# Attention and a squared-ReLU FFN: two units' rest rows stored and multiplied as one pair in the last unit, a new order of the second product, piece differences on VectorE

## The chip, the core and the metric

The kernel runs on one core of a Trainium2 chip. Its time is the device time of one execution in microseconds; "before" is the median of three runs. Five engines work side by side, each through its own instructions in order: TensorE (PE, matrix products into the eight PSUM banks; PEld are its weight loads), VectorE (DVE), ScalarE (ACT), GpSimd (POOL) and SyncE (SP), which here issues nearly all DMAs.

## What is computed

```python
# q, k, v: (8, 12, 448, 64); g_q, g_k: (64,); w_in: (768, 2048); w_out: (2048, 768); all fp32
q_n, k_n = rmsnorm(q, g_q), rmsnorm(k, g_k)
attn = softmax(q_n @ k_n^T / sqrt(64))
x = (attn @ v) as (3584, 768)          # 8 batches of 448 tokens, 12 heads of 64
h = maximum(x @ w_in, 0)
out = (h * h) @ w_out
```

## The kernel before

The eight batches form four **units** of two batches (u = 0 to 3). While a unit's FFN runs, the attention of the next two batches is worked in between: `run` draws pieces of the FFN from a generator (`ffn`) until a planned cost is spent, then a **visit** puts in the attention of the next pair of heads (`visit_among`, `visit_whole`). `place` gives the cost at which each visit comes; in units 1 and 2 there are three visits to each block. The last unit (u = 3) has no attention beside it.

A unit's FFN has four **blocks** (`NBLK`), each with a quarter of the hidden features. A block has two stages:

- The **first product** x @ w_in. Unit 0 uses seven products in place of eight on 2 x 2 parts (`first_products`, matmuls of 448 columns, L971); units 1 to 3 apply the same scheme twice (`deep_products`, matmuls of 224 columns, L1027). The weights for that, ten pieces each of seven forms, are derived in unit 0 (`deep_steps`, `derive`): ten sums for each of four blocks and each of two slices of forms, five and five, L1403. Two of each five (pieces 5 and 9) run on POOL, three on DVE. Each result goes into one of four buffers ("more") and is stored to DRAM by SP (L1421) before the buffer is used again; one step is taken at each `yield` of the stream.
- The **second product** (h*h) @ w_out (`second_products`). Tokens of a batch are 448 = 3 x 128 + 64. For each of three token tiles `tt` the first batch's 128 tokens and the second batch's are the upper and lower half of a seven-product scheme (P1 to P7, table `PRODUCTS`, L1212, each product two contraction steps of 128x384). Its left operands S1, S2, S4 and S3 are sums that POOL makes of the hidden values (`hidden_sum`, L1136). The results are added by DVE into accumulators in SBUF (`add_to`, L1269 and L1239; in a unit's first block ACT or DVE copies instead).
- The **rests**, 64 tokens of each batch, together 128 rows, are multiplied plainly: four parts by two halves of columns, eight matmuls a block (`multiply_rest`, L1150), into an accumulator of their own.

In units 1 to 3 the first tile of a block follows `FIRST_OF_BLOCK = P1, rest0, P5, P4, P6, P2, rest1, P3, P7`, where the two rest steps use banks 1 and 2 and stand where POOL still makes the sums; the other tiles follow `SECOND_ORDER = P1, P2, P5, P6, P4, P3, P7`. Three banks serve the products by turns (`roles`). P1 is issued before the last step of the first product. The tasks of attention on POOL and elsewhere are held back until the sums, or the rests, are through (`held`).

SP's queue has the loads of attention, of weights (`load_piece` L891, `load_out` L901) and the stores of results (`store`, L1274) in the order in which the program issues them; `later` delays an issue by a number of steps. An engine's queue is in order: a waiting instruction holds those behind it.

Of the kernel before, what the change touches and what calls it, by code (L numbers as in the profile page):

```python
# [14 lines left out]
F32 = mybir.dt.float32  # L15
# [3 lines left out]
ALU = mybir.AluOpType  # L19
# [3 lines left out]
P = 128  # L23
# [201 lines left out]
def program(ctx, tc, rows, v, g, wide, ones, moe_w_in, moe_w_out, out, shift):  # L225

    nc = tc.nc
# [687 lines left out]
    FIRST_ORDER = ["P1", "P5", "P2", "P6", "P3", "P4", "P7"]  # L915
    FIRST_OF_BLOCK = ["P1", "rest0", "P5", "P4", "P6", "P2", "rest1", "P3", "P7"]
    SECOND_ORDER = ["P1", "P2", "P5", "P6", "P4", "P3", "P7"]
    COST_IN, COST_OUT, COST_DEEP = 12 * NK // 2, 10, 3
    COST_SECOND = (NT * 7 + 4) * COST_OUT
    COST = NF // 2 * 7 * COST_IN + NBLK * COST_SECOND  # L920
    LATER = NBLK * (7 * 11 * COST_DEEP + COST_SECOND)

# [6 lines left out]
    def ffn(u):  # L931

        accs = []
        for blk in range(NBLK):

            hid = [
                ffn_p.tile([P, 2, 2, S], F32, name="hid", tag=f"hid{a}", bufs=1) for a in range(2)
            ]
            sums_ = [
                ffn_p.tile([P, 2, NT * P], F32, name="sums", tag=f"S{n}", bufs=1) for n in range(3)  # L940
            ]
            second = second_products(u, blk, hid, sums_, accs)
            if u:
                yield from deep_products(u, blk, hid, sums_, second)
            else:
                for t in range(2):
                    products = first_products(u, 2 * blk + t, [a[:, t] for a in hid])
                    for n, cost in enumerate(products):
                        if t and n < 4:
                            hidden_sum(hid, sums_, 0, n)  # L950
                        if t and blk == NBLK - 1:
                            let_go(u, PRODUCTS[FIRST_ORDER[n]][3])
                        yield cost
                make_all_deep()
                if blk == NBLK - 1:
                    for n in range(4):
                        load_piece(n, False)
                        load_piece(n, True)
            yield from second
# [184 lines left out]
    def multiply_rest(u, blk, hid, places, some, acc=None, halves=range(2)):  # L1144

        w_sb = [out_sb[n] for n in out_of(u, blk)]
        for half in halves:
# [7 lines left out]
            if acc is not None:  # L1155
                add_to(acc[:, ts(half, HALF)], ps, blk == 0)

    def second_products(u, blk, hid, sums_, accs):

        if blk == 0:  # L1160
            accs.extend(new_acc() for _ in range(2 * NT + 1))
        flat = [a.rearrange("p t e s -> p t (e s)") for a in hid]
        ns = out_of(u, blk)
        w_sb = [out_sb[n] for n in ns]
# [14 lines left out]
            turn_roles(2, 1, 0)  # L1179

        def store_rows(tt, e):
            if tt is None:
                parts = [(2 * u, P * NT, REST), (2 * u + 1, 0, REST)]
            else:
                parts = [(2 * u + e, REST * e + P * tt, P)]
            store(accs[-1 if tt is None else 2 * tt + e], parts)

        to_store = deque([(None, 0)])
        final = u == B // 2 - 1
        (a11, s3), (a12, a22) = [(a[:, :, LOWER], a[:, :, UPPER]) for a in flat]  # L1190
        lefts = {"11": a11, "12": a12, "22": a22, "S1": s1, "S2": s2, "S3": s3, "S4": s4}
        for tt in range(NT):
            upper_acc, lower_acc = accs[2 * tt], accs[2 * tt + 1]
            c11, c12 = [upper_acc[:, ts(h, HALF)] for h in range(2)]
            c21, c22 = [lower_acc[:, ts(h, HALF)] for h in range(2)]
            order = SECOND_ORDER if tt or not u else FIRST_OF_BLOCK
            engine = nc.scalar if order is SECOND_ORDER else nc.vector
            for name in order:
                if name.startswith("rest"):
                    a = int(name[-1])  # L1200
# [5 lines left out]
                        held.discard("others")  # L1206
                    yield 2 * COST_OUT
                    continue
                role, first, left, right = PRODUCTS[name]
                ps = roles[role][:, 0:HALF]  # L1210
                for t in range(2):
                    nc.tensor.matmul(  # L1212
                        ps, lhsT=lefts[left][:, t, ts(tt, P)], rhs=w_sb[t][:, OUT.index(right), :],
                        start=first and t == 0, stop=t == 1,
                        skip_group_check=not first,
                    )
                if name == "P1":
                    add_to(c11, ps, blk == 0, engine)
                    if order is FIRST_OF_BLOCK:
                        make_sums(0, 1)  # L1220
                        yield COST_OUT
                        make_sums(2, 3)
                        held.discard("pool")
                        continue
                elif name == "P5":
                    add_to(c22, ps, blk == 0, engine)
                elif name == "P2":
                    add_to(c11, ps)
                elif name == "P6":
                    add_to(c12, ps, blk == 0, engine)  # L1230
                elif name == "P4":
                    if blk == 0 and engine is nc.scalar:
                        nc.scalar.mul(c21, ps, -1.0)
                    elif blk == 0:
                        nc.vector.tensor_scalar(
                            out=c21, in0=ps, scalar1=-1.0, scalar2=None, op0=ALU.mult
                        )
                    else:
                        nc.vector.tensor_tensor(out=c21, in0=c21, in1=ps, op=ALU.subtract)  # L1239
                elif name == "P3":  # L1240
                    add_to(c12, ps)
                else:
                    add_to(c21, ps)
                    add_to(c22, ps)
                    to_store.append((tt, 1))
                if name == "P3":
                    to_store.append((tt, 0))
                if name in ("P2", "P4") and blk == NBLK - 1:
                    while to_store and order is not FIRST_OF_BLOCK:
                        store_rows(*to_store.popleft())  # L1250
                yield COST_OUT
            turn_roles(2, 0, 1)
        while to_store and blk == NBLK - 1:
# [132 lines left out]
    def deep_steps(blk, upper, lower):  # L1386
# [11 lines left out]
        def derive(some, n, left, right, op):  # L1398
            size = some.stop - some.start
            made[n] = ffn_p.tile([P, 4, P], F32, name="more", tag="more", bufs=4)[:, 0:size]  # L1400
            left, right = [x() for x in (left, right)]
            engine = nc.gpsimd if n in (5, 9) else nc.vector
            engine.tensor_tensor(out=made[n], in0=left, in1=right, op=op)  # L1403
            to_keep.append((keep[:, some, PLACES[n]], made[n]))

        to_keep, steps = deque(), []
# [94 lines left out]
    def place(u, x):  # L1501
# [1 line left out]
        if u == 0:  # L1503
            return COST * x / unit
        block = LATER // NBLK
        second = block - COST_SECOND
        offsets = (second * 3 // 7, second + 9 * COST_OUT, second + 22 * COST_OUT)
        at = [0] + [b * block + some for b in range(NBLK) for some in offsets]
        at[-1] = LATER
        n, more = divmod(x / VISITS, 1)  # L1510
# [67 lines left out]
    def new_acc():  # L1578
        return ffn_p.tile([P, DM], F32, name="acc", tag="acc", bufs=2 * NT + 1)
# [247 lines left out]
```

## Time and profile before

| | us |
|---|---|
| time, median of three runs (1410.63 to 1413.95) | 1411.15 |
| time of the profiled execution | 1414.61 |
| its span, first to last instruction | 1412.7 |
| ACT busy (42%) | 587.9 |
| POOL busy (57%) | 802.0 |
| matmuls of first products L971 and L1027 (xT) | 131.6 and 289.5 |
| matmuls of second products L1212 (hid and sums) | 271.3 and 205.6 |

The span is counted from the first instruction; stretches and starts are in us from there. Unit 0's FFN lies at about 110 to 500, unit 1's at 505 to 835, unit 2's at 835 to 1160 and unit 3's at 1160 to 1407. An fp32 matmul leaves two records each of PE and PEld. Records of PE overlap, so a row's mean is longer than the distance from one to the next.

DMA sizes and times to landing, from the list of DMA issues: out_sb 1536 KB 9.7 us; in_sb 384 KB 4.0 us; x_rows 224 KB 3.7 us; out_dram 384 KB 3.1 us and 192 KB 2.8 us; in_deep from "more" 256 KB 2.8 us and 192 KB 3.8 us.

### The profile page before, as it was taken

Reading aid. Unit: us, or ns where it says so; the run is one execution under the profiler, and the core shown is the slowest. Engines: PE = TensorE matmul, PEld = TensorE weight load, DVE = VectorE, ACT = ScalarE, POOL = GpSimd, SP = SyncE. Lnnn points to the kernel's source line nnn. Section 1 sums busy time; section 2 is a strip of 40 time slices with the busy share of each in tenths; the row PEclk is TensorE's granted clock in tenths of the full one; section 3 lists DMA queues with packets and bytes.
Section 4 is the critical chain, followed back from the end, with each engine's and each line's share of the span. In section 5 each row is a group of like instructions: output and inputs, shape, how many; then the busy total and the mean of one; then the engine's idle time right before and its main releaser. Section 6 shows DMA issues by size and latency. Waiting matters only on the chain.

```text
span 1412.7 us, 19458 instructions
## 1 busy us (share of the span) xinstructions
PE 1373.6 (97%) x6336; PEld 849.9 (60%) x6336; DVE 847.8 (60%) x1659; ACT 587.9 (42%) x1126; POOL 802.0 (57%) x794
## 2 busy tenths in 40 slices
PE   7999999999999999999999999999999999999998
PEld 3333444444444466685766767576676868778694
DVE  4998565987888764355455765454554564344443
ACT  6775566645646234442343434343342403121230
POOL 5668855755756877475575877565574554030311
PEclk9999999999999999999999999999999999999999
DMA  5556746867759875382646747374641726324132
GB/s 144 144 146 179 202 106 170 234 176 195 241 136 267 253 219 167 76 267 66 198 134 200 186 122 257 85 206 123 189 136 44 254 71 231 126 91 175 45 146 81
DMA packets 378931, 229.15 MB, mean 162 GB/s; under 512 B 271940, under 2 KB 347588, under 8 KB 374724
## 3 DMA queue, kind: packets, MB, share of 16 engines
q1 hardware_dynamic: 378528, 227.75, 55.6%
q8 instruction: 52, 0.85, 0.2%
q14 instruction: 59, 0.48, 0.1%
q10 hardware_dynamic: 292, 0.07, 0.0%
HBM read 172.49 MB, written 55.25 MB: 161 GB/s over the span
## 4 chain that ended last, share of the span: by engine, by line
PE 78%; POOL 5%; issue 4%; DMA 4%; DVE 3%; SPq 2%; ACT 2%; POOLq 0%; DVEq 0%; ACTq 0%
PE bank L1212 30%; PE bank L1027 20%; PE bank L971 7%; PE bank L1150 5%; PE bank L549 4%; PE bank L434 4%; PE bank L445 4%; PE bank L535 3%; POOL sum L472 2%; DMA words<-in_moe_w_in_dram 1%; DMA qk<-in_k_dram 1%; DMA words<-in_moe_w_out_dram 1%; POOL rr L203 1%; PE bank L610 1%; PE bank L570 1%
## 5 line engine op out<-in xcount | busy, mean ns | idle before, releaser
L1027 PE MATMUL bank<-xT,in_sb 128*128 128x224 f32 x1344 | 289.5, 354 | 5.1 <-ACT part L1016 2.5
L1212 PE MATMUL bank<-out_sb,hid 128*128 128x384 f32 x768 | 271.3, 490 | 6.6 <-DVE acc L1269 4.8
L1269 DVE TENSOR_TENSOR acc<-acc,bank 128x384 f32<-128x384 f32 x324 | 173.3, 549 | 170.6 <-PE bank L1212 141.2
L1027 PEld LDWEIGHTS bank<-xT,in_sb 128*128 128x128 f32 x1344 | 252.5, 190 | 17.4 <-ACT wT L453 5.6
L453 ACT ACTIVATE wT<-bank,rr 128x448 f32<-128x448 f32 x288 | 164.4, 632 | 170.7 <-PE bank L434 99.9
L1212 PEld LDWEIGHTS bank<-out_sb,hid 128*128 128x128 f32 x768 | 144.9, 191 | 111.9 <-DVE acc L1269 8.6
L1212 PE MATMUL bank<-out_sb,sums 128*128 128x384 f32 x576 | 205.6, 489 | 1.5 <-DVE acc L1269 1.4
L203 POOL TENSOR_TENSOR rr<-ms,minus_half 128x8 f32<-128x8 f32 (+1 forms) x96 | 147.3, 1535 | 76.6 <-DVE ms L196 73.1
L1012 DVE TENSOR_TENSOR hid<-hid,bank 128x224 f32<-128x224 f32 x312 | 111.1, 383 | 86.4 <-PE bank L1027 82.5
L1212 PEld LDWEIGHTS bank<-out_sb,sums 128*128 128x128 f32 x576 | 107.9, 190 | 85.4 <-issue 4.8
L971 PE MATMUL bank<-xT,in_sb 128*128 128x448 f32 x336 | 131.6, 545 | 0.0
L472 POOL TENSOR_TENSOR sum<-sum,wT 128x448 f32<-128x448 f32 (+1 forms) x96 | 112.1, 1189 | 9.6 <-ACT wT L453 8.1
L1080 POOL TENSOR_TENSOR hid<-hid 128x448 f32<-128x448 f32 x24 | 27.3, 1144 | 158.2 <-DVE hid L1012 153.8
L445 PE MATMUL bank<-qT,kT 64*128 64x448 f32 (+1 forms) x492 | 104.6, 571 | 3.5 <-ACT qT L368 2.0
L472 POOL TENSOR_TENSOR sum<-wT 128x448 f32<-128x448 f32 x48 | 57.5, 1220 | 88.3 <-ACT wT L453 88.3
L971 PEld LDWEIGHTS bank<-xT,in_sb 128*128 128x128 f32 x336 | 62.2, 190 | 68.6 <-issue 62.8
L1150 PE MATMUL bank<-out_sb,hid 128*128 128x384 f32 x256 | 87.6, 488 | 0.0
L1084 ACT ACTIVATE hid<-hid 128x448 f32<-128x448 f32 x96 | 55.0, 573 | 69.6 <-DVE hid L1012 48.5
L1027 PE MATMUL bank<-more,in_sb 128*128 128x224 f32 x288 | 76.1, 357 | 1.5 <-DVE hid L1022 1.5
L434 PE MATMUL bank<-qT,kT 64*64 64x448 f32 x552 | 75.7, 541 | 1.9 <-ACT wT L453 1.9
L180 ACT ACTIVATE squares<-qk 128x512 f32<-128x512 f32 (+1 forms) x68 | 39.4, 579 | 88.6 <-POOL xT L689 51.1
L445 PEld LDWEIGHTS bank<-qT,kT 64*128 64x128 f32 (+1 forms) x492 | 35.8, 166 | 65.7 <-issue 40.8
(136 smaller groups left out, 2037.5 us busy)
## 6 DMA issues: line engine op xcount, KB each, us to landing
out_sb<-out_forms SPq DMA_DIRECT2D x24, 1536.0 KB, 9.7
in_sb<-in_deep SPq DMA_DIRECT2D x64, 384.0 KB, 4.0
in_sb<-in_deep SPq DMA_DIRECT2D x80, 256.0 KB, 3.9
words<-in_moe_w_in_dram SPq DMA_DIRECT2D x32, 384.0 KB, 3.6
words<-in_moe_w_out_dram SPq DMA_DIRECT2D x32, 384.0 KB, 3.6
out_forms<-out_sb SPq DMA_DIRECT2D x8, 1536.0 KB, 6.8
qk<-in_q_dram SPq DMA_DIRECT2D x96, 96.0 KB, 2.6
qk<-in_k_dram SPq DMA_DIRECT2D x96, 96.0 KB, 2.7
```

The costliest lines, as they stand in the source:

```text
L203: self.nc.gpsimd.tensor_tensor(out=self.rr[i][:, x, 0 : self.count(i)], in0=ms, in1=self.minus_half.to_broadcast(list(ms.shape)), op=ALU.pow,)
L434: nc.tensor.matmul(sc[ds(half * D, D)], lhsT=turned[i, 1][ds(e * D, D), ds(m * P + half * D, D)], rhs=turned[i, 0][ds(e * D, D), :], start ...
L445: nc.tensor.matmul(sc[some], lhsT=turned[p, 1][r, keys], rhs=turned[p, 0][r, :], start=True, stop=True,)
L453: nc.scalar.activation(new_weights((i, m), e), sc, AF.Exp, scale=rows.rr[i][:, 1, 2 * m + e : 2 * m + e + 1],)
L472: nc.gpsimd.tensor_tensor(out=sums[i, e][some], in0=left[some], in1=weights[key_of(i, m), e][some], op=ALU.add)
L549: nc.tensor.matmul(bank[ds(e * D, D), :], lhsT=values[i][keys, n, e, :], rhs=weights[(i, n), e][keys], start=n == 0, stop=n == NJ - 1 and ...
L971: nc.tensor.matmul(ps, lhsT=w_sb[:, IN.index(left), c, :], rhs=forms[u, c][right], start=first and c == 0, stop=c == NK - 1, skip_group_ch ...
L1012: nc.vector.tensor_tensor(out=quarter(name, n), in0=quarter(base, n), in1=ps, op=ALU.add)
L1027: nc.tensor.matmul(ps, lhsT=left, rhs=right, start=start, stop=stop, skip_group_check=True)
L1150: nc.tensor.matmul(ps, lhsT=hid[a].rearrange("p t e s -> p t (e s)")[:, t, ds(NT * P, P)], rhs=w_sb[t][:, 2 * a + half, :], start=(a, t) = ...
L1212: nc.tensor.matmul(ps, lhsT=lefts[left][:, t, ts(tt, P)], rhs=w_sb[t][:, OUT.index(right), :], start=first and t == 0, stop=t == 1, skip_g ...
L1269: nc.vector.tensor_tensor(out=acc, in0=acc, in1=ps, op=ALU.add)
```

## The change

Three things change.

1. **Rests of units 1 and 2** (`KEPT`) are no longer multiplied there. `keep_rests` stores the 128 rest columns of both hidden tiles to DRAM, two DMAs of 128 KB for each block. In the last unit `bring_rests` loads the same block's rests of both units at the block's start into tiles that attention no longer uses, and `add_rests` makes the four sums on POOL (128x256). The rests of unit 1 are the upper half and those of unit 2 the lower half of a fourth tile (`tt == NT`), which runs the seven products in `SECOND_ORDER` behind the three others. Its accumulators lie in the tiles of q and k rows, and its rows are stored at the end. Units 0 and 3 multiply their own rests as before.
2. **Units 1 and 2 follow `SPLIT_ORDER`**, 21 products of all three tiles in one list, each with a number of its bank: five banks (the three of `roles` and banks 1 and 2) until P2 of the first tile, then three, while one of the five goes back to attention in exchange (`roles[:], banks[1] = ...`). The costs in `place` follow: visits come at 7 and 18 products after the first product's end instead of 9 and 22.
3. **Pieces 5 and 9** in `derive` run on DVE instead of POOL: 16 sums of 128x512 and 128x384.

```diff
+    SPLIT_ORDER = [
+        ("P1", 0, 0), ("P1", 1, 3), ("P4", 0, 2), ("P5", 0, 1), ("P4", 1, 4), ("P6", 0, 0),
+        ("P2", 0, 2), ("P3", 0, 1), ("P7", 0, 0), ("P6", 1, 3), ("P2", 1, 1), ("P5", 1, 0),
+        ("P1", 2, 1), ("P3", 1, 0), ("P7", 1, 3), ("P2", 2, 0), ("P6", 2, 1), ("P5", 2, 3),
+        ("P4", 2, 0), ("P3", 2, 3), ("P7", 2, 1),
+    ]
-    LATER = NBLK * (7 * 11 * COST_DEEP + COST_SECOND)
+    COST_SHORT = NT * 7 * COST_OUT
+    LATER = NBLK * (7 * 11 * COST_DEEP + COST_SHORT)
+    KEPT = range(1, B // 2 - 1)
+    kept = {u: dram.tile([NBLK, P, 2, 2, P], F32, name=f"rests{u}") for u in KEPT}
+    extra = {}
...
             second = second_products(u, blk, hid, sums_, accs)
+            if u == B // 2 - 1:
+                bring_rests(blk)
+                add_rests()
...
+    def keep_rests(u, blk, hid):
+        for a in range(2):
+            nc.sync.dma_start(
+                kept[u][blk, :, a],
+                hid[a].rearrange("p t e s -> p t (e s)")[:, :, ds(NT * P, P)],
+            )
+    def bring_rests(blk):
+        if not extra:
+            for name in ("11", "12", "S3", "22", "S1", "S2", "S4"):
+                some = att.tile([P, S], F32, name="wT", tag="wT", bufs=8)
+                extra[name] = some[:, 0 : 2 * P].rearrange("p (t n) -> p t n", t=2)
...
+        for u, names in zip(KEPT, (("11", "12"), ("S3", "22"))):
+            for a, name in enumerate(names):
+                nc.sync.dma_start(extra[name], kept[u][blk, :, a])
+    def add_rests():
...
+            (s1, a21, a22, ALU.add), (s2, s1, a11, ALU.subtract),
+            (s4, a12, s2, ALU.subtract), (a21, a11, a21, ALU.subtract),
+        ):
+            nc.gpsimd.tensor_tensor(out=dst, in0=left, in1=right, op=op)
...
+        if split:
+            places = [*roles, banks[1], banks[2]]
+            for name, tt, n in SPLIT_ORDER:
+                engine = nc.scalar if tt and n < 3 else nc.vector
+                product(tt, name, places[n][:, 0:HALF], engine)
+                if (name, tt) == ("P1", 0):
+                    yield from sums_behind_first()
+                    continue
+                if (name, tt) == ("P2", 0):
+                    roles[:], banks[1] = [places[0], places[3], places[1]], places[2]
+                    held.discard("others")
+                    later.append([3, lambda: keep_rests(u, blk, hid)])
+                if tt:
+                    store_some(name)
+                yield COST_OUT
+        for tt in range(0 if split else NT + final):
...
-            engine = nc.gpsimd if n in (5, 9) else nc.vector
-            engine.tensor_tensor(out=made[n], in0=left, in1=right, op=op)
+            nc.vector.tensor_tensor(out=made[n], in0=left, in1=right, op=op)
...
-        second = block - COST_SECOND
-        offsets = (second * 3 // 7, second + 9 * COST_OUT, second + 22 * COST_OUT)
+        second = block - COST_SHORT
+        offsets = (second * 3 // 7, second + 7 * COST_OUT, second + 18 * COST_OUT)
```

## The prediction

> **What bounds the kernel now.** I read the engine totals first, then the chain of waits, then the engines' busy time stretch by stretch, and last the timeline where something waits.
>
> ```profile
> span 1412.7 us, 19458 instructions
> PE 1373.6 (97%) x6336; PEld 849.9 (60%) x6336; DVE 847.8 (60%) x1659; ACT 587.9 (42%) x1126; POOL 802.0 (57%) x794
> L1150 PE MATMUL bank<-out_sb,hid 128*128 128x384 f32 x256 | 87.6, 488 | 0.0
> ```
>
> PE is the bound over the whole span: 97%. The L1150 row is the rests' multiplication, the work that the change cuts: 256 records in four units of four blocks, 16 in each block (8 matmuls, two records to each fp32 matmul). Its mean of 488 ns is not what one costs, since matmuls overlap; the chain of waits in the last unit gives that:
>
> ```profile
> 1262.83 20.64 PE bank L1212 x64
> 1283.47 28.55 PE bank L1027 x150
> 1324.39 20.64 PE bank L1212 x64
> ```
>
> 64 records of 128x384 back to back take 20.64 us, 0.3225 us each. These rows join without a gap: a block of the last unit is pure PE time (1262.83 to 1324.39, 61.56 us). By stretch:
>
> ```profile
> 345.00:369.00 24.00, 21.96 (x75) 8.75 (x74) 23.59 (x32) 17.09 (x34) 22.34 (x18) 1.00 0.88 252
> 440.00:462.00 22.00, 22.00 (x74) 9.65 (x73) 21.59 (x30) 12.60 (x24) 16.99 (x16) 1.00 0.94 279
> 600.00:700.00 100.00, 99.08 (x556) 70.42 (x555) 52.35 (x112) 38.06 (x73) 58.91 (x58) 1.00 0.63 183
> 1200.00:1300.00 100.00, 100.00 (x410) 77.14 (x410) 41.35 (x88) 19.75 (x41) 12.98 (x12) 1.00 0.35 126
> ```
>
> Columns: stretch, its length, then busy PE, PEld, DVE, ACT, POOL. In the second unit (600 to 700) PE is 99% busy with DVE at half; in the last PE is full. Only in the first unit is another engine full: DVE is busy 98% of 345 to 369 and 440 to 462, and there PE does wait:
>
> ```profile
> PE bank L1212 <- DVE acc L1269: 6.2, 5, 2.2
> PE bank L445 <- ACT qT L368: 2.0, 1, 2.0
> PE bank L1212 <- POOL out_sb L1443: 1.8, 1, 1.8
> ```
>
> All of these lie in the first unit: 277.39 (0.31), 281.66 (1.42), 285.76 (2.17), 380.22 (0.92) and 469.61 (1.43) for the accumulators, 367.81 for qT, 472.30 for out_sb.
>
> **The product count (part 1).** Units 2 and 3 lose their rests: 2 units x 4 blocks x 16 = 128 records x 0.3225 = 41.28 us. The last unit gains one pair by seven products: 4 blocks x 7 products x 2 contraction steps x 2 records = 112 x 0.3225 = 36.12 us. Net -16 records, **-5.16 us**. Both sides stand on the path at full price: in units 2 and 3 PE is 98 to 99% busy, in the last unit 100%. Seven products for eight is all that the arithmetic can give.
>
> **What part 1 adds elsewhere.** Stores: 2 per block of two units, 128 KB each, 16 in all, on SP. They read hid, which the next block writes first about 14 products (18 us) and a whole attention visit later; x_rows stores of 224 KB land in 3.7 us. SP does block (10.5 us from 570.12), but the stores stand ahead of that load in the new order. Loads: 4 per block of the last unit, 128 KB; in_sb loads of 128 KB land in 3.0 us. In blocks 2 to 4 they wait at SP for the previous pair to leave PE, and the in_sb loads queued behind them are four to five pieces ahead of PE (a piece is 22 records, 4.2 us), so some 16 us cover them. POOL: 4 sums of 128x256 per block, at most the 1.0 us of the 128x384 rows (L1136), so 4 us, used first about 56 us later. Only in the first block do T3 and T4 pieces (L718, until 1167.8) queue behind them and the load: 3 us + 4 us takes them to about 1175, and PE needs T3 at its sixth piece, 1160.2 + 5 x 4.2 = 1181. Cover 6 us. DVE: 8 evictions of 0.55 us in 9.03 us of PE, 4.4 us: hidden. Tail: the last row store becomes two of 192 KB (2.8 us to landing) for one of 384 KB (3.1); one more issue at some 0.4 us against 0.3 us. Together **0**, ends 0 and +1.5.
>
> **The new order of the second product (part 2).** PE has no stall in the old second products of units 2 and 3 above the 0.7 us restart after a visit, so nothing can be gained. What can be lost is bank reuse. Eviction time:
>
> ```profile
> 554.92 1.45 PE L1212 MATMUL bank<-out_sb,sums 128*128 128x384 f32 x4
> 556.41 0.56 DVE L1267 COPY acc<-bank 128x384 f32<-128x384 f32 x1 [1.27 <-PE bank L1212]
> ```
>
> From a product's first matmul to the end of its eviction is 2.05 us (556.97 - 554.92). The old order always had two other products (2 x 1.29 us) between two uses of a bank: free 1.8 us early. The new order has only one between P2 and P1 of the next tile, P5 and P3, P3 and P2: reuse at 2.58 us, 0.5 us early. That is 3 places x 8 blocks = 24. DVE runs strictly in order, so whatever stands ahead of these evictions counts: the qT and kT transposes (two of 0.6 us), a reduce with its scaling (0.55 + 0.17), the transposes of the inverse (0.65, held by POOL: at 659.57 it waited 1.08). Following the new order, most long ones fall after an eviction that has two products of room; the transposes after P2 put P5's eviction 0.5 us late, just at the margin. Two thirds of the places keep their margin and one third loses about 0.1 us: **+1**. Ends: 0, and 24 x 0.25 = +6 if DVE is typically 0.7 us late. The sums for P5, P6, P3 and P7 come no later relative to PE: P5 still stands 2.58 us behind P1's neighbour (two products instead of half the rests), and the visit now lies between P2 and P3, so S4 (ready at 557.5) and S3 (559.4) are in time. Visits come 2.6 us closer twice a block; POOL, which feeds them, idles 4.5 to 7.6 us before each, so it stays covered, and if not, each visit could cost the missing part (in the +6).
>
> **Piece differences (part 3).** 16 sums leave POOL (mean 1.3 us, 21 us) for DVE. What one costs on DVE: 0.55 us alone, 0.65 median, so 16 x 0.6 = 9.7 us more on an engine that is full in two stretches. Against it stands what POOL's sums do to DVE:
>
> ```profile
> 350.09 1.58 POOL L1403 TENSOR_TENSOR more<-in_sb 128x512 f32<-128x512 f32 x1
> 350.46 1.42 DVE L1342 TENSOR_SCALAR out_sb<-words 128x384 uint32<-128x384 uint32 x1
> 351.81 0.61 DVE L1113 TENSOR_TENSOR hid<-bank,part 128x448 f32<-128x448 f32 x1
> ```
>
> L1342's median is 0.354 us; beside a POOL sum it took 1.42, while L1113, which reads PSUM, kept its 0.61. Summed over all DVE instructions that overlap a POOL piece, time above their usual duration is 16.4 us: 1 us per piece. In 345 to 369: relief 4.6 us, added 2.4; in 440 to 462: 4.1 against 2.4; around 259 to 272: 2.0 against 1.8. So DVE reaches qT of 367.81 some 2.2 us sooner (PE's wait of 2.0 goes; next late there is PE itself) and the accumulator of 469.61 1.7 us sooner (1.4 goes; the wait for out_sb at 472.30 hangs on POOL sums behind ACT and stays). Sum -3.4.
>
> Two rules of the Trainium skill speak against this step. Perfetto Trace Analysis, section Optimizing Scalar/DVE Operations, says that where VectorE is saturated, work may be given away, even to GpSimd; this change takes it back into 98% busy stretches: by that rule +2.4 us in each of three blocks, +7.2. SBUF — State Buffer, section Who interferes with whom, says that a VectorE instruction with two SBUF inputs and a GpSimd one that reads SBUF exclude each other for the whole instruction: the moved sums have two such inputs and would wait on POOL's remaining work (1.35 us at 355.91 instead of 0.55). At 1.35 each, 16 cost 21.6, against the relief of 16.4: +5.2. The medians of the 24 piece sums already on DVE (0.65) say that most escape; I take the rows.
>
> And one loss, in the first block:
>
> ```profile
> 152.29 0.24 DVE L660 RECIPROCAL few<-inverse 128x14 f32<-128x14 f32 x1
> 156.20 1.09 SPq L1421 DMA_DIRECT2D in_deep<-more  x2
> 157.84 1.16 DVE L1113 TENSOR_TENSOR hid<-bank,part 128x448 f32<-128x448 f32 x2 [3.90 <-PE bank L971]
> 159.08 1.27 POOL L1403 TENSOR_TENSOR more<-in_sb 128x512 f32<-128x512 f32 x1 [5.72 <-DMA in_deep<-more]
> ```
>
> The fifth piece reuses a buffer and waits until 159.08 for a store. On DVE it stands ahead of L660: reciprocal, transpose and xT (1.5 us), then the two L1113, which end at about 162.4 instead of 159.0. Their bank is wanted by P2, the third product behind (157.4 + 2 x 2.26 = 161.9): **+0.6**, ends 0 and +3. Part 3: -3.4 + 0.6 = -2.8, taken as **-2.5** since a wait that goes often shows later; ends -5 and +9.
>
> **Sum.** -5.2 + 0 + 1 - 2.5 = -6.7 us. The profiled execution took 1414.61 us (span 1412.7 and 1.9 around it) and becomes 1407.9. It lies 3.5 above the median shown, 1411.15, which becomes **1404.5**.
>
> **Rivals.**
> (a) The evictions decide: the 24 close reuses cost 0.25 us each. For: DVE backlogs exist (P6's accumulation at 660.14 began 0.9 us late). Against: most evictions start at once (0.73 idle before them). Then -5.2 + 6 - 2.5 = -1.7: 1409.5.
> (b) VectorE becomes the bound of the first unit, and the kernel is slower. Place: 250 to 290, 345 to 382, 440 to 475 and the buffer wait of 152 to 159. Price: three blocks x 2.4 us without relief, and 2.5 in the first, 9.7. For: the 98% rows. Against: the relief just counted. It decides from 5.2 us lost there: -5.2 + 9.7 = +4.5: 1415.7.
> (c) The first unit gains more: the waits at 281 and 285 (3.6 us) go as well, and part 2 costs nothing: -5.2 - 5 = -10: 1401.
> That the count is not what it says is excluded: PE loses 8 matmuls in the built order, 16 records.
>
> **Numbers.** Likeliest 0.55 (own range 1401.5 to 1407.5), (a) 0.20, (b) 0.09, (c) 0.16. A measurement of this kernel tells 0.3% (4.2 us) from no change: faster is below 1406.9. Faster: 0.55 x 0.9 + 0.16 + 0.2 x 0.2 = 0.70; slower (b) 0.09; the rest 0.21. The range, 1399.5 to 1410.5, takes in (a) and most of (c).
>
> **What would show it.** Right: L1150 with 128 records, 112 more in the second product; blocks of the last unit 61.56 + 9.03 = 70.6 us with no gap; DVE rows of 1.2 to 1.4 us beside 350 gone; no wait at 367. Wrong: PE waits on accumulators in units 2 and 3 (the close reuses), a PE gap near 162, or waits in the first unit that add up to more than the 12 us of now.

## The result, and the profile after

| | before | after |
|---|---|---|
| median, us (twelve runs each, same chip) | 1411.95 | 1407.65 |
| ratio | | 0.9973, 95% interval 0.9961 to 0.9985 |
| the ratio as a difference, us | | -3.8 (-5.5 to -2.1) |
| profiled execution and its span, us | 1414.61 / 1412.7 | 1412.59 / 1410.8 |

1407.65 us lies in the predicted range, 3.1 us above the predicted 1404.5. The interval lies wholly below 1; but by the prediction's own bound of 0.3% (a ratio of 0.997) a ratio of 0.9973 is no change that can be told, where a chance of 0.70 was put on faster. The differences in us in what follows are made from the ratios, as here; the two medians themselves lie 4.3 us apart.

The page of after, engine totals and the group of the new sums (busy time and count; then idle time in front and what ended it):

```profile
span 1410.8 us, 19536 instructions
PE 1374.5 (97%) x6320; PEld 848.1 (60%) x6320; DVE 856.9 (61%) x1699; ACT 583.4 (41%) x1118; POOL 795.0 (56%) x794
...
L1202 POOL TENSOR_TENSOR wT<-wT 128x256 f32<-128x256 f32 x16 | 11.5, 729 | 104.9 <-DMA wT<-rests 104.2
```

PE has the 16 records less (6336 to 6320) that the sum was made with. POOL's 104 us of waiting for the loaded rests are idle time and cost nothing: its 16 sums are 0.73 us each.

The groups of after by shape, rests (now L1164) and the pair:

```profile
L1164 PE MATMUL bank<-out_sb,hid 128*128 128x384 f32 x128 | 43.7, 489 | 0.0
L1250 PE MATMUL bank<-out_sb,wT 128*128 128x384 f32 x112 | 36.8, 486 | 0.0
```

128 records of rests are left, 112 have come, none with idle time in front. The chain of work that ended last, of after, in the last unit (start, length, records):

```profile
1262.01 28.55 PE bank L1041 x150
...
1295.19 5.16 PE bank L1250 x16
...
1302.93 29.67 PE bank L1250 x92
1332.60 28.55 PE bank L1041 x150
```

A block now lasts from 1262.01 to 1332.60, 70.59 us, where it was 61.56: 9.03 more, and the rows still join.

Where the time went is read from the first matmul of each block's first product in the trace, the distance from one block to the next (us). In before the four units' first blocks start at 134.56, 512.09, 841.86 and 1160.17. What the change and the kernel number 0 to 3 is called the first to the last unit here; the prediction's "units 2 and 3" are the second and the third.

| stretch | before | after |
|---|---|---|
| first unit, four blocks | 91.41, 95.90, 91.30, 98.92 | 91.87, 96.34, 90.60, 99.67 |
| second unit, four blocks | 83.80, 81.85, 82.03, 82.09 | 78.10, 76.65, 76.80, 77.96 |
| third unit, four blocks | 83.49, 81.85, 82.06, 70.91 | 78.47, 76.68, 76.86, 65.76 |
| last unit: three blocks; fourth, to PE's last matmul | 61.57, 61.57, 61.56; 61.23 | 70.59, 70.60, 70.59; 70.27 |
| PE's last matmul to the end | 6.65 | 8.08 |

The second and third unit lose 40.8 us, the last gains 36.1, the end 1.4, and the first unit did not get shorter at all in this execution. Its waits did; here the waits of PE in after's first unit (100 to 514; total, times, longest):

```profile
PE bank L1250 <- DVE acc L1344: 5.6, 6, 1.5
PE bank L434 <- ACT wT L453: 1.9, 1, 1.9
...
PE bank L1250 <- POOL out_sb L1517: 0.7, 1, 0.7
PE bank L445 <- ACT qT L368: 0.6, 1, 0.6
```

The wait for qT fell from 2.0 to 0.6, that for out_sb from 1.8 to 0.7, those for the accumulators from 6.2 to 5.6. Two matters stand in the way of seeing that in the unit's length: the clock (next fence), and VectorE, which is as full as before (experiment 4). Stretches of after: length, busy PE, PEld, DVE, ACT, POOL, granted clock:

```profile
345.00:369.00 24.00, 23.41 (x79) 9.41 (x78) 23.55 (x36) 18.28 (x37) 16.81 (x14) 1.00 0.91 263
413.70:513.37 99.67, 95.57 (x339) 43.08 (x337) 72.44 (x125) 45.01 (x85) 69.85 (x64) 0.97 0.77 216
284.00:290.80 6.80, 6.21 (x12) 2.22 (x14) 5.63 (x10) 1.58 (x3) 3.59 (x3) 0.50 0.66 165
```

In the full stretch VectorE is still busy 23.55 of 24.00 us, now with 36 instructions for 32; POOL went from 22.34 to 16.81. The last row is a stretch in which TensorE's granted clock was 0.50. After had four such stretches of 3.4 us in the first unit (two at 284, one at 471.8, one at 509.3), before had two (285.2 and 473.0); the last section takes them up. The timeline where VectorE's rows of 1.2 to 1.4 us had been forecast to go:

```profile
350.03 1.45 POOL L1150 TENSOR_TENSOR sums<-sums,hid 128x384 f32<-128x384 f32 x1
350.55 1.35 DVE L1437 SCALAR_TENSOR_TENSOR out_sb<-words,out_sb 128x384 uint32<-128x384 uint32 x1
351.44 1.31 POOL L1517 TENSOR_TENSOR out_sb<-out_sb 128x384 f32<-128x384 f32 x1
```

They are still there. The piece's sum has left POOL, and the next POOL sum has taken its place beside VectorE. In the first block stands the loss that the prediction had named:

```profile
159.38 0.69 DVE L1477 TENSOR_TENSOR more<-in_sb 128x512 f32<-128x512 f32 x1 [6.51 <-DMA in_deep<-more]
159.99 0.24 DVE L660 RECIPROCAL few<-inverse 128x14 f32<-128x14 f32 x1
...
162.76 2.52 PE L985 MATMUL bank<-xT,in_sb 128*128 128x448 f32 x6 [0.19 <-DVE hid L1127]
```

The fifth piece waits for its buffer's store, and L660, which ran at 152.29 before, waits behind it in VectorE's queue. Last, the end of before:

```profile
1405.92 2.09 SPq L1274 DMA_DIRECT2D out_dram<-acc  x2
1406.63 1.02 DVE L1269 TENSOR_TENSOR acc<-acc,bank 128x384 f32<-128x384 f32 x2 [0.73 <-PE bank L1212]
```

and of after:

```profile
1402.51 3.65 SPq L1349 DMA_DIRECT2D out_dram<-qk  x4
1403.22 1.02 DVE L1344 TENSOR_TENSOR qk<-qk,bank 128x384 f32<-128x384 f32 x2 [0.73 <-PE bank L1250]
```

The last rows leave as four stores of 64 rows, each accumulator in two; two of the four can be issued only behind the last eviction (1404.24), at 1404.27 and 1404.79. Before, one store of 128 rows stood there. Its issue took 0.33 us and it landed 3.1 us behind the eviction; the last of after took 1.38 us to issue and landed 4.2 us behind it.

### The profile page after: what moved, and what is told of

Same layout as the page of the kernel before. It is cut to its first block, busy times and chain, and to the rows that moved or that the text cites. A ratio compares the mean times of both kernels' runs of the same rounds, so it can differ in the third digit from the quotient of the medians.

```text
span 1410.8 us, 19536 instructions
## 1 busy us (share of the span) xinstructions
PE 1374.5 (97%) x6320; PEld 848.1 (60%) x6320; DVE 856.9 (61%) x1699; ACT 583.4 (41%) x1118; POOL 795.0 (56%) x794
## 4 chain that ended last, share of the span: by engine, by line
PE 62%; DVE 3%; POOL 3%; issue 2%; SPq 2%; DMA 1%; ACT 1%; DVEq 0%; POOLq 0%; ACTq 0%
PE bank L1250 27%; PE bank L1041 20%; PE bank L549 4%; PE bank L434 4%; PE bank L1164 2%; POOL sum L472 2%; PE bank L445 1%; PE bank L985 1%; SPq L325 1%; PE bank L610 1%; PE bank L535 1%; DMA in_sb<-in_deep 1%; PE bank L570 1%; POOL xT L689 0%; DVE ms L193 0%
## 5 line engine op out<-in xcount | busy, mean ns | idle before, releaser
L1250 PE MATMUL bank<-out_sb,hid 128*128 128x384 f32 x768 | 274.8, 491 | 4.5 <-DVE acc L1344 3.8
L1344 DVE TENSOR_TENSOR acc<-acc,bank 128x384 f32<-128x384 f32 x312 | 166.4, 548 | 150.2 <-PE bank L1250 134.6
L549 PE MATMUL bank<-wT,vt 64*64 64x448 f32 x576 | 74.3, 548 | 0.0
L368 ACT ACTIVATE qT<-qT,g 128x448 f32<-128x448 f32 x34 | 22.7, 667 | 121.2 <-DVE qT L366 121.2
L1202 POOL TENSOR_TENSOR wT<-wT 128x256 f32<-128x256 f32 x16 | 11.5, 729 | 104.9 <-DMA wT<-rests 104.2
```

The lines of the kernel that those rows point to most:

```text
L549: nc.tensor.matmul(bank[ds(e * D, D), :], lhsT=values[i][keys, n, e, :], rhs=weights[(i, n), e][keys], start=n == 0, stop=n == NJ - 1 and ...
L1250: nc.tensor.matmul(ps, lhsT=extra[left][:, t] if tt == NT else lefts[left][:, t, ts(tt, P)], rhs=w_sb[t][:, OUT.index(right), :], start=fi ...
L1344: nc.vector.tensor_tensor(out=acc, in0=acc, in1=ps, op=ALU.add)
```

## The experiments

Ratios are to the kernel before on the same chip, in one series of runs. Blocks are the distances of the table above.

### 1. The parts apart: pieces alone, and all but the pieces

`pieces_only` is before with this edit; `no_pieces` is the change with its reverse.

```diff
-            engine = nc.gpsimd if n in (5, 9) else nc.vector
-            engine.tensor_tensor(out=made[n], in0=left, in1=right, op=op)
+            nc.vector.tensor_tensor(out=made[n], in0=left, in1=right, op=op)
```

> Only the third part: pieces 5 and 9 on VectorE, all else as before. Theory 1 (the step of the prediction stands): the waits of the first unit shrink by about 3 us (the wait for qT near 367 goes from 2.0 to about 0.6, that for out_sb near 472 from 1.8 to 0.7, a new one of about 0.4 near 162): 2.4 us faster than before, ratio about 0.998. Theory 2 (the relief is only a shift, the time comes back later in the first unit): the second unit starts at the same time as before, within 0.5 us, ratio 1.000. In both the tail behind the last matmul stays at 6.65 us.

> The changed kernel with pieces 5 and 9 back on GpSimd: parts one and two alone. Theory 1: blocks of units 1 and 2 are 5.1 us shorter, blocks of the last unit 9.03 us longer, tail 1.4 us longer, the first unit as before: -40.8 + 36.1 + 1.4 = -3.3 us, ratio 0.9977, some 2.4 us slower than the changed kernel. Theory 2 (part three gains nothing): the same time as the changed kernel.

Measured: the pieces alone 0.9975 (0.9962 to 0.9988), -3.5 us; all but the pieces 0.9962 (0.9947 to 0.9976), -5.4 us. The blocks of the second to the last unit were those of before and of the change, to within the waits for in_sb loads (the third unit's first block 83.93 and 77.74), and the end was 6.62 and 8.48 us: so the longer end belongs to the pair, not to the pieces. But -3.5 and -5.4 don't add up to the -3.8 of the change, which had been measured in another series, and both are larger than their forecasts, -2.4 and -3.3. Either the pieces lose beside the other parts, or series can't be set against each other to 2 us. Experiment 4 takes that up.

### 2. The pair third in place of last

```diff
-        for tt in range(0 if split else NT + final):
+        for tt in [] if split else [0, 1, NT, 2] if final else range(NT):
```

> The changed kernel with the pair of rests multiplied before the last tile of the last unit, so that the last stores are two of 128 rows again instead of four of 64. Theory 1 (the tail's 1.4 us come from four small stores at the end): from the last matmul's start to the end 6.65 us as before instead of 8.08, 1.4 us faster than the changed kernel, ratio to before about 0.996. Theory 2 (the tail is longer by chance of one execution, or by the pair's accumulators): tail stays near 8 us, no gain.

Measured: 0.9943 (0.9929 to 0.9958), -8.1 us, where 0.996 was forecast. The end of its timeline:

```profile
1397.26 2.09 SPq L1349 DMA_DIRECT2D out_dram<-acc  x2
1397.96 1.02 DVE L1344 TENSOR_TENSOR acc<-acc,bank 128x384 f32<-128x384 f32 x2 [0.73 <-PE bank L1250]
```

Two stores in place of four, and 6.64 us from the last matmul to the end where the change has 8.08. The blocks are the same (70.59 to 70.60). So the end's loss goes with the stores that come last: the length of the end came as forecast, the ratio did not.

### 3. What the new order is worth

The rests dropped as in the change, but the second and third unit left in the old order:

```diff
-        if split:
+        if False:
...
-        for tt in range(0 if split else NT + final):
+        for tt in range(NT + final):
...
+                if name.startswith("rest") and split:
+                    continue
...
+                if name == "P2" and split and tt == 0:
+                    held.discard("others")
+                    later.append([3, lambda: keep_rests(u, blk, hid)])
```

> The changed kernel, but the first tile of units 1 and 2 keeps the order P1, P5, P4, P6, P2, P3, P7 of before with the rest steps left out, and the other tiles their old order in three banks. Theory 1 (the new list is what replaces the rests as cover for GpSimd's sums): P5 would stand where rest0 stood, 0.1 us before S1 is ready, P2 0.2 us before its input, P7 0.6 us before S3: about 1 us of waits a block, 8 us in eight blocks, so about 4 us slower than before, ratio 1.003. Theory 2 (the sums were not close, the order is free): ratio as the changed kernel, 0.997; then blocks of units 1 and 2 are near 76.7 us, with theory 1 near 77.7.

Measured: 1.0074 (1.0055 to 1.0093), 10.5 us **slower** than before. The eight blocks take 77.8 to 80.2 us (the last 69.37), together 16.3 us more than in the pair-third version: theory 1's direction at twice its size. The end is 7.34 us here; the fourth store's issue took 0.64 us, where it took 1.4 to 1.8 in the other versions with the pair last. The timeline at the start of a second product, loads of weights beside matmuls:

```profile
624.82 2.38 POOL L1150 TENSOR_TENSOR sums<-hid 128x384 f32<-128x384 f32 x2 [0.95 <-ACT hid L1099]
...
625.88 0.30 PEld L1250 LDWEIGHTS bank<-out_sb,sums 128*128 128x128 f32 x2 [0.84 <-POOL sums L1150]
625.88 0.91 PE L1250 MATMUL bank<-out_sb,sums 128*128 128x384 f32 x2 [0.50 <-POOL sums L1150]
...
627.25 0.30 PEld L1250 LDWEIGHTS bank<-out_sb,sums 128*128 128x128 f32 x2 [1.08 <-POOL sums L1150]
```

PE's own row shows half of the wait: the weight load waits for the sum, and PE for the load. P5 needs S1, which POOL begins at 624.82, and each of its two contraction steps takes POOL 1.2 us and PE 0.65. Counted from matmul to matmul, 13.35 of the 16.3 us lie in the second products and in front of them, 1.67 a block; the other 3.0 lie at attention's products of q and k. Before, the rests' first half stood there, 8 records of work that needs no sum:

```profile
550.28 2.07 POOL L1136 TENSOR_TENSOR sums<-hid 128x384 f32<-128x384 f32 x2 [0.96 <-ACT hid L1085]
...
552.34 2.74 PE L1150 MATMUL bank<-out_sb,hid 128*128 128x384 f32 x8
```

P5 followed at 554.92 without a wait (its row is in the prediction).

That any product would do as cover was the next thought. P4 needs no sum:

```diff
+    AHEAD = ["P1", "P4", "P5", "P6", "P2", "P3", "P7"]
...
-            order = SECOND_ORDER if tt or not u else FIRST_OF_BLOCK
+            order = SECOND_ORDER if tt or not u else AHEAD if split else FIRST_OF_BLOCK
```

> The second and third unit in the old order without rest steps, but with P4 put ahead of P5 in a block's first tile (P1, P4, P5, P6, P2, P3, P7). In the old order without rests, PE stood still behind GpSimd's sums at the start of every second product: 1.67 us a block in the eight blocks (13.35 of the 16.3 us by which they were longer than in the new order). Theory 1 (the rests, and in the new order the second tile's P1 and two P4, cover these sums): one product of 1.29 us more stands ahead of the first sum, S1 comes with no wait and S2 with some 0.36 us, so the eight blocks lose 1.0 to 1.3 us each against the old order, 8 to 10.5 in all; time 8 to 10.5 us below the 1.0074 of before, ratio 1.0000 to 1.0017. Theory 2 (the old order loses by where its visits and held tasks fall, not by the sums): less than 3 us gained, ratio 1.0053 to 1.0074.

Measured: 1.010 (1.0082 to 1.0119), nothing gained in time; the blocks are 15.1 us over the new order's, 1.2 less than without P4. The forecast of 8 to 10.5 fell:

```profile
626.44 2.38 POOL L1151 TENSOR_TENSOR sums<-hid 128x384 f32<-128x384 f32 x2 [0.94 <-ACT hid L1100]
...
627.58 1.53 PE L1251 MATMUL bank<-out_sb,hid 128*128 128x384 f32 x4 [0.57 <-ACT hid L1100]
```

P4's left operand is the hidden half that ACT squares last. PE waited for ACT in place of POOL, and the sums, which start from the same half, still came too late for what follows. P4 began 2.8 us behind P1, as P5 had without it (2.7), and two weight loads behind it still waited for sums (0.44 us at 630.22 and 0.66 at 631.17). The new order has the second tile's P1 in this place, whose operand is the half that is ready:

```diff
+            if split and tt == 1:
+                roles[0] = ahead
...
                     yield from sums_behind_first()
+                    if split:
+                        ahead = banks[1]
+                        product(1, "P1", ahead[:, 0:HALF], nc.scalar)
+                        yield COST_OUT
...
+                    banks[1] = roles[2]
```

> The old order without rest steps, with the second tile's P1 put behind the first tile's P1 in a bank that attention lends and gets back. With P4 in that place the blocks were no shorter than in the old order: P4's left operand is the hidden half that ScalarE squares last, so PE waited for that (8.9 us between the first product's end and P4 in place of 7.7) and the sums came late all the same. The second tile's P1 reads the half that is ready. Theory 1 (a product whose operand is ready, not any product, must cover the sums; this is what the rests did before and what the second P1 does in the new order): 1.29 us of cover ahead of P5 and, with P4 behind P5, enough for S2 too, so the wait of 1.67 us a block goes: eight blocks together 11 to 13.5 us shorter than in the old order (excess over the new order 16.3 falls to 3 to 5), ratio 0.998 to 0.9997. Theory 2 (visits and held tasks): less than 4 us gained, ratio above 1.0045.

Measured: 0.9992 (0.998 to 1.0005). The eight blocks are 4.1 us over the new order's, 12.2 of the 16.3 are back. The same place in its timeline:

```profile
623.66 2.38 POOL L1150 TENSOR_TENSOR sums<-hid 128x384 f32<-128x384 f32 x2 [0.95 <-ACT hid L1099]
...
624.06 1.45 PE L1250 MATMUL bank<-out_sb,hid 128*128 128x384 f32 x4
...
625.35 1.66 PE L1250 MATMUL bank<-out_sb,sums 128*128 128x384 f32 x4
...
626.10 0.30 PEld L1250 LDWEIGHTS bank<-out_sb,sums 128*128 128x128 f32 x2 [0.55 <-POOL sums L1150]
```

The second tile's P1 (624.06) stands where PE had stood still, and of the 0.84 and 1.08 us of waiting 0.55 is left, most of it beside running matmuls. The 3.0 us at the products of q and k are gone as well; the 4.1 that are left lie in the second products. So the rests had been covering POOL's sums, and the new order earns its keep by putting other ready work there.

### 4. The pieces and the end, four kernels on one chip

The change, and each of its two variants, and both together.

> The change as it is, beside the three variants on one chip. Its terms by the traces so far: product count -5.2 us, close bank reuse +0.5, tail +1.4, piece differences on VectorE -1.2 to -2.5. Theory 1 (these terms add): -4.5 to -5.8 us against the kernel before, ratio 0.9959 to 0.9968. Theory 2 (beside the other parts, the pieces on VectorE bring nothing or cost up to 1.5 us, as the earlier ratios 0.9973 with and 0.9962 without them suggest): -3.3 to -1.8, ratio 0.9977 to 0.9987, and slower than the variant without them by 0 to 1.5 us.

> The change with piece differences 5 and 9 back on GpSimd, on the same chip as the change itself. Theory 1: slower than the change by 1.2 to 2.5 us, ratio to the kernel before 0.9973 to 0.9977. Theory 2: not slower than the change, ratio 0.9962 to 0.9977 and at or below that of the change.

> The change with the pair put third in the last unit's blocks, so that two 128-row stores end the kernel. Both theories: the tail of 6.6 us in place of 8.1 to 8.5, so 1.4 to 1.8 us faster than the change on the same chip. If the tail were covered by something else, no difference. The earlier ratio was 0.9943; by theory 1 it is now 0.9947 to 0.9957.

> The pair third and piece differences 5 and 9 on GpSimd: the second pair for the worth of the pieces, free of the tail. Theory 1: slower than the pair-third version with them on VectorE by 1.2 to 2.5 us, and no wait of 1.2 us or more in the first unit is gained; the waits for qT (2.0 us) and for the accumulator behind it (1.4) are back. Theory 2: equal to it or faster by up to 1.5 us.

| us, same chip (before 1412.71, 53 runs) | pieces on VectorE | pieces 5 and 9 on GpSimd |
|---|---|---|
| pair last | 1409.10, ratio 0.9974 (0.9963 to 0.9985) | 1410.54, 0.9981 (0.9973 to 0.9988) |
| pair third | 1407.63, ratio 0.9958 (0.9941 to 0.9975) | 1408.96, 0.9973 (0.9962 to 0.9983) |

Across, the pieces are worth 1.4 and 1.3 us; down, the pair third 1.5 and 1.6. Single intervals overlap, but both pairs say the same (from both pairs together, by resampling the runs, the 95% intervals are 0.7 to 2.5 us for the pieces and 0.4 to 2.3 for the pair's place), and the lower ends of theory 1's terms (1.2 and 1.4) are met. The forecast ratios were missed: theory 1 had 0.9959 to 0.9968 for the change and theory 2 0.9977 to 0.9987, and 0.9974 lies between; `no_pieces` and the pair third lie just above theory 1's ranges too (0.9981 against 0.9977, 0.9958 against 0.9957). So the differences between the four kernels speak for theory 1, their distance from before does not. The -5.4 of `no_pieces` in the earlier series is -2.7 (-3.8 to -1.7) here: the discrepancy was between series. In the earlier one the runs of before had a mean granted clock of 0.9958, those of `no_pieces` 0.9967 and of the pair third 0.9973, so that a part of those ratios may be clock (last section). The gain of the change itself came out the same, -3.7 us (-5.2 to -2.1).

The blocks say where the pieces pay, compared between executions in which the same number of stretches of half clock fell into the block: with the pieces on VectorE the first block takes 91.7 to 92.0 against 91.4, the second 93.99 against 94.50, the third 90.6 against 91.3, the fourth 98.47 against 98.91 (one stretch in each of these two). Together -1.2.

Which waits make this up is seen when the matmuls of the two pair-third versions are matched one by one. PE's idle time before a matmul in us, where it is above 0.25 us between 228 and 500 (the starts are those of the version with pieces 5 and 9 on GpSimd):

| at, waiting for | pieces 5 and 9 on GpSimd | all on VectorE |
|---|---|---|
| 277.8, accumulator | 0.31 | 0.63 |
| 282.1, accumulator | 1.41 | 1.53 |
| 286.2, accumulator | 2.17 | 1.23 |
| 366.9, qT | 2.04 | 0.59 |
| 376.9, accumulator | none | 0.29 |
| 379.3, accumulator | 0.91 | 1.12 |
| 468.6, accumulator | 1.42 | 1.44 |
| 471.3, out_sb | 1.77 | 0.68 |

Three waits shrink, by 3.5 us in all, and others grow or are new. By the starts of matmuls the three give back 3.3 us, five places behind or ahead of them take 1.7 (at 278, 377, 379, 463 and 487), and 162 takes 0.3: what PE won at one wait it lost by half at the next.

Why VectorE could not do better is in its busy time, over the first unit's four blocks, the same work in both. First the pair third with pieces on GpSimd, stretch and then VectorE's two shapes of piece sums that concern the move:

```profile
134.98:511.11 376.13, 363.92 (x1228) 166.96 (x1224) 277.04 (x468) 200.31 (x384) 250.59 (x212) 1.00 0.71 193
...
L1478 DVE TENSOR_TENSOR more<-in_sb 128x512 f32<-128x512 f32 x4 | 3.0, 752 | 0.0
L1478 DVE TENSOR_TENSOR more<-in_sb 128x384 f32<-128x384 f32 x4 | 3.2, 805 | 0.9 <-DMA in_deep<-more 0.9
L1437 DVE SCALAR_TENSOR_TENSOR out_sb<-words,out_sb 128x384 uint32<-128x384 uint32 x24 | 20.1, 838 | 0.0
```

and the pair third with all pieces on VectorE:

```profile
134.31:509.14 374.83, 365.01 (x1229) 166.80 (x1225) 281.00 (x484) 200.15 (x384) 234.70 (x198) 1.00 0.72 195
...
L1477 DVE TENSOR_TENSOR more<-in_sb 128x512 f32<-128x512 f32 x12 | 10.5, 877 | 6.4 <-DMA in_deep<-more 6.4
L1477 DVE TENSOR_TENSOR more<-in_sb 128x384 f32<-128x384 f32 x12 | 9.7, 806 | 1.7 <-DMA in_deep<-more 1.7
L1437 DVE SCALAR_TENSOR_TENSOR out_sb<-words,out_sb 128x384 uint32<-128x384 uint32 x24 | 16.3, 679 | 0.0
```

The 16 moved sums add 7.5 + 6.5 = 14.0 us to VectorE, 0.875 each. VectorE's total rises by 281.00 - 277.04 = 4.0, so the other rows take 10.0 less of it (8.4 by adding their durations, since VectorE's records overlap in part; 3.8 of it L1437's, as the last rows show). Where the relief stopped can be counted: 31 rows of VectorE, other than pieces, ran beside one of POOL's pieces and stood 12.2 us above the medians of their kinds. With the pieces moved, 16 of the 31 run for over half their length beside another POOL instruction; these held 9.7 of the 12.2 us and gave back 2.9. VectorE has more to do than before, and PE's waits get shorter all the same; that the rows they wait for stand behind the relieved ones and ahead of some of the added ones is the likely reason, and was not tested.

### 5. The pieces of the first block back on GpSimd

```diff
-            nc.vector.tensor_tensor(out=made[n], in0=left, in1=right, op=op)
+            engine = nc.gpsimd if n in (5, 9) and blk == 0 else nc.vector
+            engine.tensor_tensor(out=made[n], in0=left, in1=right, op=op)
```

> The pair third, and piece differences 5 and 9 of the first weight block on GpSimd as before, those of the other three blocks on VectorE. In the variants with all of them on VectorE the first block of the first unit took 91.75 to 91.92 us, in those with none 91.40 to 91.41. Theory 1 (the fifth piece, waiting for its buffer, holds VectorE): the first block returns to 91.4 and the three others keep 94.0 (without a stretch of half clock), 90.6 and their wait for qT of 0.6, so 0.4 us is won, a ratio of about 0.995 that can't be told from the pair-third version's by time alone. Theory 2 (the 0.4 is a matter of chance or comes from elsewhere): the first block stays at 91.8.

Measured: 0.997 (0.9957 to 0.9983), where about 0.995 was forecast; by time not told apart from the pair third with all pieces on VectorE. The first block took 91.41, the third 90.61; the second took 96.40, with two stretches of half clock in it. Against the pair third the first block's matmuls start at the same distances up to 162, there the pair third falls 0.34 us behind, and it stays so to the block's end. That the fifth piece's wait for its buffer costs some 0.4 us in the first block is borne out by the trace, and is too little for the time.

## Why the prediction was right in kind and off in size

- **The product count (part 1), -5.16.** Right, on both sides: +9.03 per block in the last unit, and the second and third unit 40.8 us shorter in the profiled execution, 42.0 in experiment 4's, where 40.3 had been forecast (41.28 less 1 for close reuse). Of these, waits for in_sb loads take a share that changes from execution to execution (before 2.5 us, after 1.3, then none); set aside, they leave 39.6 and 39.5.
- **Close bank reuse (part 2), +1.** About right in size: 41.28 - 39.6 = 1.7 by the blocks, of which 1.0 are named waits for accumulators in the second and third unit (0.6 for DVE, 0.4 for ACT); the other 0.7 has no name. Rival (a), 0.25 us at each of 24 places, is out. The places were miscounted, though: `SPLIT_ORDER` has four a block, since P3 of the third tile also comes two products behind the P5 whose bank it uses. The waits are not spread over them; they are three, all before a P3: twice in the second tile (574.29 and 884.17, 0.2 us each, for ACT) and once, the longest (814.47, 0.65 us, for DVE), at the place that was not counted.
- **"Nothing can be gained" by the new order (part 2).** True against the order of before and misleading as a price: the order is what makes part 1 worth its -5.2. With the old order the whole change is 10.5 us slower than before (experiment 3). The prediction had the reason in its hands (P5 still stands 2.58 us behind) but put no price on the rests as cover.
- **What part 1 adds elsewhere, 0.** Its end of +1.5 came, not 0: the term for the tail was mis-sized. One more issue of 0.4 us and a landing time of 2.8 were put against 0.3 and 3.1. The extra store came, but the last one is issued 0.5 us behind its neighbour, for 1.38 us, and lands 3.7 us after its start, so the end lies 1.4 us later (8.08 against 6.65). Why that issue takes so long was not tested. Stores and loads of rests, POOL's sums and the evictions did cost nothing.
- **The pieces (part 3), -2.5.** The term was mis-sized by half: -1.2 by the blocks, -1.3 and -1.4 by the two pairs of times. The step that failed is "relief of 16.4 us for 9.7 added". The relief measured 8.4 to 10.0, since much of what had run beside a piece now runs beside another POOL sum (experiment 4); an added sum costs 0.875 us and not 0.6. (The 16.4 itself, added again from the trace of before, comes to 13.8 with the medians as the usual times and to 15.0 with the shortest.) The waits named were right in part, and their sum by luck: that for qT fell by 1.4 of 2.0; that for the accumulator at 469.61, which was to go, stayed (1.42 and 1.44 in experiment 4), and that for out_sb at 472.30, which was to stay, fell by 1.1. The reserve "a wait that goes often shows later" was the right thought, but took 0.3 off where half came back. The +0.6 in the first block was right (0.3 to 0.6, all of it at 162), and the rows of 1.2 to 1.4 us beside 350 stayed.
- **The two rules held against part 3.** The Trainium skill's page SBUF — State Buffer, section Who interferes with whom, says that a sum with two SBUF inputs on VectorE contends with GpSimd's reads, over a port pair that is locked exclusively. The prediction priced that at 1.35 us each and set it aside for the medians; the 0.875 lies between the two. Its +5.2, which is 21.6 added less 16.4, did not come: PE's waits shrank while VectorE's load grew. Nor did the +7.2 come that it drew from the page Perfetto Trace Analysis, section Optimizing Scalar/DVE Operations; that section goes on to say that moving work between these two engines might not help, since they share a read port. Here the move the other way was worth 1.3 to 1.4 us.
- **Rivals.** (b), VectorE as the bound and slower, did not happen: the first unit's waits fell. (c) needed the waits at 281 and 285 to go; the second fell by 0.9, the first did not fall. Of the signs of being wrong two came, both small: waits for accumulators in the second and third unit (1.0 us) and PE's wait near 162.

With the measured terms: -40.8 + 36.1 + 1.4 - 1.2 = -4.5 us, against measured -3.8 (-5.5 to -2.1) and -3.7 (-5.2 to -2.1). The rest of 0.7 us is inside the intervals, and the share of the in_sb waits (1.2 of the 40.8) is of its size. Of the 3 us that the forecast of -6.7 is short, 1.4 are the end and 1.3 the pieces.

The version that beats both kernels is the pair third: 0.9943 (0.9929 to 0.9958) and 0.9958 (0.9941 to 0.9975) in two series.

## What to carry to other kernels

Before cutting work from a full engine, ask what runs in its shadow: here the rests hid another engine's sums, and the cut without new cover made the kernel slower. A cover is only as good as its own operand: of two products that need no sum, the one whose input was ready closed the gap and the other waited for something else. Work that is moved off an engine which disturbs a second one can give back less than its neighbours' lost time, since the next instruction of the disturber may take its place; here 8.4 to 10.0 us came of a reckoned 16.4. And what was stored last in fewer issues ended sooner.

## What the runs showed of the hardware

**One kernel, two lengths.** The profiled spans of the change differ by 5.9 us between two executions, 1410.8 at a mean clock of 0.994 and 1404.9 at 0.999. The second execution over the same two blocks of the first unit:

```profile
227.32:321.31 93.99, 90.50 (x298) 41.13 (x296) 76.66 (x130) 53.88 (x105) 53.37 (x43) 1.00 0.74 202
411.92:508.69 96.77, 92.66 (x338) 42.05 (x336) 73.72 (x125) 44.93 (x85) 68.26 (x62) 1.00 0.77 220
```

At a clock of 1.00 these blocks take 93.99 and 96.77 us, with stretches of half clock 96.34 and 99.67: 5.25 of the 5.9 us, for four stretches of 3.4 us. They start at distances that are multiples of 3.41 us. Three of them follow a window of that length in which PE was busy about half the time; the fourth, at 287.4, follows at once on the one at 284.0. The three windows:

```profile
280.60:284.00 3.40, 1.74 (x6) 0.54 (x5) 3.40 (x5) 1.53 (x3) 2.76 (x4) 1.00 0.89 201
468.40:471.80 3.40, 1.53 (x4) 0.30 (x3) 1.98 (x3) 0.00 (x0) 3.24 (x4) 0.99 1.07 378
505.90:509.30 3.40, 1.50 (x12) 0.44 (x12) 1.34 (x3) 2.03 (x4) 3.32 (x4) 1.00 0.35 93
```

These are the waits of 1.5 to 1.9 us for the accumulators and for wT. The Trainium skill (TensorE: Matmul & The Clock Gate, Part 1) has free-running windows of 3.4 us and half clock after an idle one; here no window was idle, PE was busy 44 to 51% of each. Not every such window was followed by half clock. On the same grid, the windows at full clock of the 13 profiled executions, from 120 to 1395 us, divide so: where PE was busy 37 to 46% of a window, half clock followed in all 13 cases; at 47 to 51% in 8 of 15 (one of the others is in before, from 507.1); at 53% and more in none. Each stretch cost 1.3 us here (5.25 over four). So a wait of 1.5 us can cost about as much again behind it, by where the windows happen to fall, and that alone is as large as the effect of the pieces. In experiment 4 the runs of before had a median of 1411.3 us at a mean clock of 0.998 and 1414.2 at 0.995, those of the change 1408.1 at 0.998 and 1412.4 at 0.994. Runs of one clock, or blocks with the same number of stretches, are what can be compared here.
